# A sparse-attention and mixer kernel: PSUM as four double tiles, the MLP in 64-row halves, one relu per pair, scores unit by unit, mask constants through POOL's DMA queue

## The chip, the core and the metric

The kernel runs on one core of a Trainium2 chip. A core has TensorE (PE: matmuls, and weight loads that run beside them), VectorE (DVE), ScalarE (ACT), GpSimd (POOL) and SyncE (SP). PE writes to PSUM, which has eight banks of 512 float32 columns on 128 partitions; ACT and DVE read it from there[...]. SP and ACT issue DMAs to a hardware queue, POOL to a software queue. The metric is the device time in microseconds (us). Each engine takes its instructions in the order in which the program has them; engines wait for each other by semaphores.

## The reference

Four batches, eight heads, 768 positions, head size 64. Attention runs with a block mask (blocks of 32: neighbours, first and last block, and three sampled blocks per row), and its output x, put back to 768 x 512, goes through a low-rank mixer and an MLP:

```
scores = q k^T / 8, masked to -1e9;  attn = softmax(scores);  x = attn v
h = x^T U V          (U: 768 x 32, V: 32 x 768)
u = x + h^T
out = u + relu(u w1) w2      (w1: 512 x 2048, w2: 2048 x 512)
```

All results are float32; the kernel multiplies in float16 and accumulates in float32.

## The kernel before, in words

The work goes through 16 head pairs (four batches of four). A pair has nine units. A unit is 1024 columns of scores on 128 partitions (keys on partitions; two heads of 512 queries, or two heads of two times 256): `scores` (line 406) writes them to a PSUM tile `psc` of two banks, one `activation` with exp (line 419) turns them into the float16 tile `est`. In batches 1 to 3 a score matmul contracts over 64 rows: head 0 lies on partitions 0 to 63, head 1 on 64 to 127, and the two are issued one after the other, on different row halves of PE. In batch 0 the mask is added inside the matmul through one-hot rows, so its score matmuls have 128 rows; in later batches `mask_mul` (line 423) multiplies `est` by a 0/1 mask `m01` on DVE.

When a pair's nine units are done, `values` (482) multiplies est by v in 72 matmuls of 65 columns (the 65th is the sum of the row) into `pav`, in two halves of three query tiles; `norm` (446) takes the reciprocal and multiplies, to `xs` (float32), and POOL casts it to `xh`. `mix_a` (496) multiplies by U into `pa`, DVE copies that to `a16`; `mix_h_rows` (532) multiplies by V in 64-row halves into `ph`, DVE adds it to xs, giving u (`xf`), POOL casts it to `uh`, and a transposing DMA (`turn_u`, 551) makes `uT`.

The MLP of a batch (`mlp_steps`, 568) is a list of steps: 32 of `w1` (one tile `pt` of 384 columns: four matmuls with 128 rows, then a relu on ACT or DVE to `tT`) and 24 of `w2` (four of the 16 matmuls of 512 columns into `pch`; after the last, DVE adds u and SP sends the result out).

The order on PE is written out at build time. Batch 0 runs its own loop (line 782). Then 108 units follow in `groups`: eight groups of one unit, then groups of two. In each group the program issues the scores, then the tail work of earlier pairs, then MLP steps of the batch before: `run_fill` (798) spreads a batch's steps over the groups up to the next entry of `OPENS`, where the next batch's MLP begins (`LATE` = 8 groups after a batch's last scores). The last batch's MLP comes after everything else. Estimates of the engines' clocks (`clk`, `run_on`, `give_back`) choose the PSUM bank and the engine of each relu while the program is built.

PSUM is two `psc` tiles of two banks each (`pscp`) and four single banks (`psp`), from which all other tiles come: `pst_tile` takes the bank that is free first.

At the start, ACT's queue loads k's first part, `small_const` (mask constants), the identity and one-hot rows; SP's queue loads q's first part, `sampled_blocks`, the rest of q and k, and so on. `small_const` and `sampled_blocks` give `eq`, `cb` and `cbd` on DVE (lines 262 to 284), from which PE makes the mask rows (`pm`, line 299).

Of the kernel before, what the change touches and what calls it, by code (L numbers as in the profile page):

```python
# [21 lines left out]
def kernel(  # L22
# [63 lines left out]
    opool = ctx.enter_context(tc.tile_pool(name="opool", bufs=2))  # L86

    pscp = ctx.enter_context(
        tc.tile_pool(name="pscp", bufs=2, space=bass.MemoryType.PSUM)
    )  # L90
    psp = ctx.enter_context(
        tc.tile_pool(name="psp", bufs=1, space=bass.MemoryType.PSUM)
    )
# [9 lines left out]
    banks = [0.0] * 4  # L103
    pairs = {"pav": deque([0, 1]), "ps": deque([2, 3])}
    held = {}

    def pst_tile(shape, dtype, name, tag=None):
        if tag is None:
            n = min(range(4), key=lambda n: banks[n])
            clk["pe"] = max(clk["pe"], banks[n])  # L110
        else:
            n = pairs[tag][0]
            pairs[tag].rotate(1)
        t = psp.tile(shape, dtype, tag=f"bank{n}", name=name)
        banks[n] = OPEN
        held[id(t)] = (n, t)
        return t

    def give_back(t, when):
        banks[held.pop(id(t))[0]] = when + LAG  # L120
# [5 lines left out]
    def mm(out, lhsT, rhs, start, stop, loose=False, us=0.0):  # L126
        clk["pe"] += us
        keep(
            nc.tensor.matmul(  # L129
                out, lhsT, rhs, start=start, stop=stop, skip_group_check=loose  # L130
            )
        )

# [85 lines left out]
    keep(nc.vector.memset(Vd, 0.0))  # L219
# [4 lines left out]
    def hot_rows(eng, st, h, n):  # L224
# [3 lines left out]
    keep(nc.sync.dma_start(out=qld[:, :, 0:TQ], in_=q0[:, :, 0:TQ]))  # L228
    keep(nc.scalar.dma_start(out=kld[:, :, 0:TK], in_=k0[:, :, 0:TK]))
    keep(  # L230
        nc.sync.dma_start(
# [4 lines left out]
    keep(nc.scalar.dma_start(out=small[0:NB], in_=small_dr.ap()))  # L236
# [85 lines left out]
    pm0 = pscp.tile([P, 2, 512], FP32, tag="psc", name="pm")  # L322
    pm1 = pst_tile([P, QA], FP32, "pm", tag="pav")
    pm2 = pscp.tile([P, 2, 512], FP32, tag="psc", name="pm")
# [33 lines left out]
    mvld = w2t[0:R, 0:3, :].rearrange("r j d -> r (j d)").bitcast(FP32)  # L358
# [47 lines left out]
    def scores(i, u, est):  # L406
        psc = pscp.tile([P, 2, 512], FP32, tag="psc", name="psc")
# [10 lines left out]
        clk["pe"] = max(clk["pe"], exp_end[-2]) + 0.32  # L418
        keep(nc.scalar.activation(out=est, in_=psc, func=AF.Exp, scale=0.125))  # L419
        exp_end.append(run_on("act", 0.905))  # L420
        ready[id(est)] = exp_end[-1]

# [23 lines left out]
    def norm(i, c, pav, xs, xh, quick=False):  # L446
# [14 lines left out]
        def full():  # L461
            times(x3)
            give_back(pav, run_on("dve", 0.48))
# [15 lines left out]
    def new_pav(tag=None):  # L479
        return pst_tile([P, 3, 2, D + 1], FP32, "pav", tag)  # L480

    def values(i, c, ests, xs, xh):
        b, hp = divmod(i, HP)
        pav = new_pav()
        for h in range(2):
            for j in range(3):
                for g in range(T):
                    mm(
                        pav[:, j, h, :],
                        weights(ests, g, 3 * c + j, h),  # L490
                        vts[b % 2][:, 2 * hp + h, g, 0 : D + 1],
                        g == 0, g == T - 1, us=0.0315,
                    )
        norm(i, c, pav, xs, xh)

    def mix_a(i, xh, box, part, tag=None):
# [4 lines left out]
        if part == 1:  # L501
            box["a"] = misc.tile([P, P], FP16, tag="a16", name="a16")
            keep(nc.vector.tensor_copy(out=box["a"], in_=box["pa"]))
            give_back(box["pa"], run_on("dve", 0.2))

    def mix_h(i, c, a16, xs, uh, tag=None, quick=False):
# [14 lines left out]
        def full():  # L521
            plus(u3)
            give_back(ph, run_on("dve", 0.47))
# [8 lines left out]
    def mix_h_rows(i, a16, xs, uh):  # L532

        b, hp = divmod(i, HP)
        phs = [pst_tile([P, 3, P], FP32, "ph") for c in range(2)]
        for j in range(3):
            for c in range(2):
                mm(phs[c][:, j, :], Vd[rows[c], 3 * c + j, :], a16[rows[c]], True, True)
        clk["pe"] += 0.17
        for c in range(2):  # L540
            tc3 = slice(3 * c, 3 * c + 3)
            u3 = xfs[b][:, tc3, hp * P : (hp + 1) * P]
            keep(
                nc.vector.tensor_tensor(  # L544
                    out=u3, in0=xs[:, tc3, :], in1=phs[c], op=ALU.add
                )
            )
            give_back(phs[c], run_on("dve", 0.47))
            keep(nc.gpsimd.tensor_copy(out=uh[:, tc3, :], in_=u3))  # L549
# [9 lines left out]
    def turn_u_pe(i, uh, tag):  # L559
# [5 lines left out]
        give_back(pt, run_on("dve", 0.6))  # L565


    def mlp_steps(b):
# [3 lines left out]
        def w1(jj, c):  # L572
            if c == 0:
                tT[jj] = tpool.tile([P, S], FP16, tag="tT", name="tT")
            uT = uTs[b].rearrange("p n t s -> p n (t s)")
            pt = pst_tile([P, HS], FP32, "pt")
            for cc in range(NCC):
                mm(
                    pt,
                    w1t[:, cc, jj * P : (jj + 1) * P],  # L580
                    uT[:, cc, c * HS : (c + 1) * HS],
                    cc == 0, cc == NCC - 1, us=0.162,
                )
            dst = tT[jj][:, c * HS : (c + 1) * HS]
            ends = {e: max(clk[e], clk["pe"]) + d for e, d in (("act", 0.43), ("dve", 0.48))}
            if ends["act"] <= ends["dve"]:
                keep(nc.scalar.activation(out=dst, in_=pt, func=AF.Relu))  # L587
                give_back(pt, run_on("act", 0.43))
            else:
                keep(nc.vector.tensor_scalar_max(out=dst, in0=pt, scalar1=0.0))  # L590
                give_back(pt, run_on("dve", 0.48))

        pchs = {}

        def w2(sc, part, n0=0, n1=HD):
            if part == 0:
                pchs[sc] = pst_tile([P, n1 - n0], FP32, "pch")
            for jj in range(4 * part, 4 * part + 4):
                mm(
                    pchs[sc],  # L600
# [4 lines left out]
            if part == 3:  # L605
                of = opool.tile([P, n1 - n0], FP32, tag="of", name="of")
                keep(
                    nc.vector.tensor_add(out=of, in0=xfs[b][:, sc, n0:n1], in1=pchs[sc])  # L608
                )
                give_back(pchs[sc], run_on("dve", 0.6))  # L610
                keep(
                    nc.sync.dma_start(
                        out=out[b].rearrange("(p t) d -> p t d", t=T)[:, sc, n0:n1],
                        in_=of,
                    )
                )

        for jj in range(NJJ):
            for c in range(2):
                steps.append((0.65, lambda jj=jj, c=c: w1(jj, c)))  # L620
        for sc in range(T):
            cuts = [(0, HD)] if (b, sc) != (B - 1, T - 1) else [(0, 384), (384, HD)]
            for n0, n1 in cuts:
                for part in range(4):
# [3 lines left out]
                            lambda sc=sc, part=part, n0=n0, n1=n1: w2(sc, part, n0, n1),  # L628
                        )
# [46 lines left out]
    def turn_part(i, nm, part):  # L676
# [4 lines left out]
        if part == 1:  # L681
# [9 lines left out]
            give_back(pt, run_on("dve", 0.48))  # L691
# [11 lines left out]
    def at_unit(i, u):  # L703
        if (i, u) in MASKS:
            mask_tiles(MASKS.index((i, u)))
        if i == 0:
            if u == 0:
# [5 lines left out]
                for nm, o, pt, t in (("q", qa[0], pq, TQ), ("k", ka[0], pk, TK)):  # L713
                    for h in range(2):
                        half_copy(nc.vector.tensor_copy, o, h, pt, t, T)
                give_back(pq, 0.0)
                give_back(pk, 0.0)
                give_back(warm, 0.0)
                issue(2, "qk")
                cast(1, "q")  # L720
                cast(1, "k")
                cast(1, "v")
            if u == 1:
                for h in range(2):
# [220 lines left out]
```

The softmax here doesn't subtract the row's maximum and nothing guards it: scores larger than these inputs give would overflow.

## Time and profile before

| what | value |
|---|---|
| runs, median of 4 (lowest, highest) | 290.3 us (290.25, 290.73) |
| the profiled execution: its own time, its span | 290.27 us, 288.40 us |
| PE busy; weight loads busy | 281.1 us (97%); 162.8 us (56%) |
| DVE, ACT, POOL busy | 188.8 (65%), 177.9 (62%), 95.8 us (33%) |
| chain that ended last, by engine | PE 84%, ACT 11%, issue, DVE and DMA 1% each |
| matmuls of pt, pch, pav, psc | 512, 400, 1152, 384 |
| exp: est<-psc on ACT | 144 of 1023 ns |
| mask: est<-est,m on DVE | 108 of 834 ns on average |
| relu on ACT, on DVE | 82 of 495 ns, 46 of 547 ns |
| TensorE's granted clock | 1.0 after the first moments |

Matmuls are pipelined: the recorded duration of one (327 ns for 384 columns) reaches past the start of the next, so the time that PE needs is read from start to start. The chain that ended last goes back from the last instruction to what released it, step by step; its shares say where the span went. Weight loads (PEld) run beside matmuls.

### The profile page before, as it was taken

The numbers are of one execution on the slowest core, as the hardware profiler recorded it, in microseconds if no ns is written. First come the engines' busy times: TensorE is split into PE (matmuls) and PEld (weight loads), VectorE is DVE, ScalarE is ACT, GpSimd is POOL, SyncE is SP. The second block draws the span as 40 slices with busy tenths as digits, with TensorE's granted clock in tenths as the row PEclk, the third lists the DMA queues.
The fourth block names the chain that finished last, engine by engine and source line by source line (L and its number), as shares of the span: only waits on it lengthen the run. The fifth ranks groups of instructions, "written<-read, shape, count | busy, mean of one in ns | idle before, by whom it ended". The sixth has DMA issues, their size and how long they took to land.

```text
span 288.4 us, 6744 instructions
## 1 busy us (share of the span) xinstructions
PE 281.1 (97%) x2765; PEld 162.8 (56%) x2765; DVE 188.8 (65%) x347; ACT 177.9 (62%) x232; POOL 95.8 (33%) x126
## 2 busy tenths in 40 slices
PE   7999998999999999999999999999999999999996
PEld 2577775456646454556565645566564644665443
DVE  5767767889897888888887695779787522000112
ACT  3699999687795857577776554577865000776000
POOL 2559854106444464516144251603031201000000
PEclk9999999999999999999999999999999999999999
DMA  6999999962357677773444365161010223000112
GB/s 168 317 286 269 235 261 268 216 188 60 84 151 97 223 165 199 217 146 67 131 124 127 99 184 137 44 93 31 0 31 0 62 77 102 36 0 2 71 74 74
DMA packets 46414, 36.91 MB, mean 128 GB/s; under 512 B 27272, under 2 KB 42896, under 8 KB 46384
## 3 DMA queue, kind: packets, MB, share of 16 engines
q1 hardware_dynamic: 43208, 32.06, 41.3%
q0 software_dynamic: 2688, 4.19, 8.1%
q8 instruction: 21, 0.34, 0.5%
q10 hardware_dynamic: 488, 0.24, 0.3%
q14 instruction: 9, 0.07, 0.1%
HBM read 27.80 MB, written 6.29 MB: 118 GB/s over the span
## 4 chain that ended last, share of the span: by engine, by line
PE 84%; ACT 11%; issue 1%; DVE 1%; DMA 1%; ACTq 0%; DVEq 0%
PE pt L129 29%; PE pch L129 29%; PE psc L129 11%; ACT est L419 11%; PE pav L129 10%; PE pa L129 2%; DMA w1t<-small_const 1%; PE ph L129 1%; PE warm L129 1%; PE pturn L194 1%; PE pm L129 0%; PE pmk L129 0%; DVE uT L564 0%; DVE xh L453 0%; PE puT L563 0%
## 5 line engine op out<-in xcount | busy, mean ns | idle before, releaser
L419 ACT ACTIVATE est<-psc 128x1024 f16<-128x1024 f32 x144 | 138.6, 1023 | 45.9 <-PE psc L129 45.3
L129 PE MATMUL pt<-uT,w1t 128*128 128x384 f16 x512 | 89.1, 327 | 0.2 <-DVE uT L564 0.2
L129 PE MATMUL pch<-w2t,tT 128*128 128x512 f16 (+2 forms) x400 | 87.9, 371 | 0.0
L431 DVE TENSOR_TENSOR est<-est,m 128x1024 f16<-128x1024 f16 x108 | 85.4, 834 | 0.0
L129 PEld LDWEIGHTS <-w1t 128*128 128x128 f16 x512 | 47.6, 98 | 38.2 <-issue 8.6
L587 ACT ACTIVATE tT<-pt 128x384 f16<-128x384 f32 x82 | 39.3, 495 | 36.1 <-PE pt L129 34.9
L129 PEld LDWEIGHTS <-tT 128*128 128x128 f16 x400 | 36.4, 98 | 44.3 <-issue 5.4
L129 PEld LDWEIGHTS <-est 128*128 128x128 f16 x1152 | 44.0, 97 | 10.8 <-issue 0.5
L471 POOL CAST xh<-xs 128x384 f16<-128x384 f32 x30 | 21.4, 716 | 85.6 <-DVE xs L453 84.8
L608 DVE TENSOR_TENSOR of<-xf,pch 128x512 f32<-128x512 f32 (+2 forms) x25 | 16.5, 661 | 49.9 <-PE pch L129 49.8
L129 PE MATMUL pav<-vt,est 128*128 128x65 f16 x1152 | 46.4, 193 | 0.1
L129 PE MATMUL psc<-qT,kT 64*128 64x512 f16 (+1 forms) x288 | 33.9, 327 | 0.9 <-ACT est L419 0.8
L549 POOL CAST uh<-xf 128x384 f16<-128x384 f32 x24 | 16.1, 696 | 38.3 <-issue 33.6
L590 DVE TENSOR_SCALAR tT<-pt 128x384 f16<-128x384 f32 x46 | 24.2, 547 | 0.9 <-PE pt L129 0.7
L129 PE MATMUL psc<-qa,ka 128*128 128x512 f16 (+1 forms) x96 | 21.6, 327 | 0.3
L453 DVE TENSOR_TENSOR xs<-pav,rcp 128x384 f32<-128x384 f32 x32 | 17.8, 557 | 1.9
L448 DVE RECIPROCAL rcp<-pav 128x6 f32<-128x6 f32 x32 | 6.2, 194 | 19.4 <-PE pav L129 18.9
L188 POOL CAST kst<-kld 128x768 f16<-128x768 f32 x15 | 16.5, 1100 | 4.3 <-DMA kld<-in_k_dram 4.3
L129 PEld LDWEIGHTS <-kT 64*128 64x128 f16 x288 | 10.2, 94 | 13.4 <-issue 8.8
L182 POOL CAST vt<-vld 128x768 f16<-128x768 f32 x16 | 15.6, 973 | 5.4 <-DMA vld<-in_v_dram 4.5
L188 POOL CAST qst<-qld 128x768 f16<-128x768 f32 x15 | 16.5, 1101 | 2.2 <-PE psc L129 1.6
L544 DVE TENSOR_TENSOR xf<-xs,ph 128x384 f32<-128x384 f32 x24 | 12.2, 548 | 4.5 <-PE ph L129 4.5
(57 smaller groups left out, 113.8 us busy)
## 6 DMA issues: line engine op xcount, KB each, us to landing
vld<-in_v_dram SPq DMA_DIRECT2D x16, 384.0 KB, 4.5
out_dram<-of SPq DMA_DIRECT2D x23, 256.0 KB, 2.2
qld<-in_q_dram SPq DMA_DIRECT2D x15, 384.0 KB, 4.5
kld<-in_k_dram SPq DMA_DIRECT2D x15, 384.0 KB, 4.0
w1t<-in_moe_w_ch_dram POOLq DMA_DIRECT2D x4, 512.0 KB, 9.8
w2t<-in_moe_w_ch_dram POOLq DMA_DIRECT2D x4, 512.0 KB, 18.4
qld<-in_q_dram SPq DMA_DIRECT2D x1, 256.0 KB, 3.2
kld<-in_k_dram SPq DMA_DIRECT2D x1, 256.0 KB, 4.2
```

Source lines behind the costliest of these rows:

```text
L129: nc.tensor.matmul(out, lhsT, rhs, start=start, stop=stop, skip_group_check=loose)
L182: nc.gpsimd.tensor_copy(out=vts[b % 2][:, 2 * hp : 2 * hp + 2, :, 0:D], in_=ld)
L188: keep(nc.gpsimd.tensor_copy(out=st.rearrange("p t h d -> p h t d"), in_=ld))
L419: keep(nc.scalar.activation(out=est, in_=psc, func=AF.Exp, scale=0.125))
L431: keep(nc.vector.tensor_tensor(out=o, in0=o, in1=m, op=ALU.mult))
L453: nc.vector.tensor_tensor(out=o.rearrange("p j (h d) -> p j h d", h=2), in0=pav[:, :, :, 0:D], in1=rcp[:, :, :, None].broadcast_to([P, 3, ...
L471: keep(nc.gpsimd.tensor_copy(out=xh[:, 3 * c : 3 * c + 3, :], in_=x3))
L544: nc.vector.tensor_tensor(out=u3, in0=xs[:, tc3, :], in1=phs[c], op=ALU.add)
L549: keep(nc.gpsimd.tensor_copy(out=uh[:, tc3, :], in_=u3))
L587: keep(nc.scalar.activation(out=dst, in_=pt, func=AF.Relu))
L590: keep(nc.vector.tensor_scalar_max(out=dst, in0=pt, scalar1=0.0))
L608: nc.vector.tensor_add(out=of, in0=xfs[b][:, sc, n0:n1], in1=pchs[sc])
```

## The change

What it does, part by part.

- PSUM: batch 0 has two double tiles of two banks (as before) and two pools of two single banks (`pav`, `ps`). Early in batch 1 (groups 6 and 7) the two single pools are closed and become two more double tiles. From then on scores, MLP pairs, values, `pa` and `ph` all take one of four doubles, the one that the planner's clocks say is free first.
- MLP of batches 0 to 2: each 128-row matmul is two of 64 rows. The two column halves (c = 0, 1) of a pair have a bank each. In phase 0, rows 0 to 63 go to bank 0 and rows 64 to 127 to bank 1; in phase 1 it is the other way round. Before phase 1, `half_wait` makes PE wait for the last matmul of phase 0 (in the built program the wait sits on the first weight load of phase 1). One relu of 768 columns per pair. `run_fill` ends a group's steps ahead of a phase 1, unless it is the group's first step. The last batch's MLP keeps 128 rows, with paired tiles and one relu per pair.
- Values: one double tile and one normalisation for a pair instead of two halves; `mix_a_rows` in 64-row halves (two sums in two banks, added on DVE); `mix_h_rows` into one double, with one add and one cast.
- Groups: one unit each; `LATE` = 14; tail steps at groups 0, 3 and 6 after a pair's last mask, instead of 0, 1, 3 and 5.
- Start: `sampled_blocks` and `small_const` are issued by POOL, first in its queue, instead of by SP and ACT. The copies of the mask rows for the second buffer (`qa`, `ka`) are issued in unit 0 instead of unit 1, ahead of pair 2's q and k. V of the mixer is loaded to two row halves; DVE's memset of `Vd` goes.
- Output: `of` holds two row tiles (one buffer instead of two), sent in one DMA in batches 0 to 2.

```diff
+    first = {
+        nm: tc.tile_pool(name=nm + "p", bufs=1, space=bass.MemoryType.PSUM, side=side)
+        for nm, side in (("ps", "left"), ("pav", "right"))
+    }
...
+    def double(name, n=None):
+        if n is None:
+            n = min(doubles, key=lambda n: doubles[n][1])
+            assert doubles[n][1] < OPEN
+            clk["pe"] = max(clk["pe"], doubles[n][1])
+        pool = doubles[n][0]
+        t = pool.tile([P, 2, 512], FP32, tag=f"double{n}", name=name)
+        doubles[n] = (pool, OPEN)
+        held[id(t)] = (n, t)
         return t
...
+    def half_wait(ins):
+        nop = nc.tensor.nop()
+        tc.add_manual_dep(
+            nop.ins, ins.ins.name,
+            mybir.DependencyInfo(mybir.DependencyClass.Sync, mybir.DependencyReason.DATA),
+            reason="halves",
+        )
+        keep(nop)
...
-    keep(nc.vector.memset(Vd, 0.0))
...
+    keep(
+        nc.gpsimd.dma_start(
+            out=sbi[0:NB].rearrange("z r w -> z (r w)"),
+            in_=sampled_blocks.bitcast(I32),
+        )
+    )
+    keep(nc.gpsimd.dma_start(out=small[0:NB], in_=small_dr.ap()))
...
-        psc = pscp.tile([P, 2, 512], FP32, tag="psc", name="psc")
+        psc = double("psc", len(exp_end) % 2 if i < HP else None)
...
+    def mix_a_rows(xh, box):
+
+        pa = double("pa")
+        for sc in range(T):
+            for r in range(2):
+                mm(
+                    pa[:, r, 0:P], Ut[rows[r], sc, :], xh[rows[r], sc, :],
+                    sc == 0, sc == T - 1, us=0.027,
+                )
+        a16 = box["a"] = misc.tile([P, P], FP16, tag="a16", name="a16")
+        keep(nc.vector.tensor_copy(out=a16, in_=pa[:, 0, 0:P]))
+        keep(nc.vector.tensor_tensor(out=a16, in0=a16, in1=pa[:, 1, 0:P], op=ALU.add))
...
-        def w1(jj, c):
-            if c == 0:
+        def w1(jj, phase, by_rows):
+            if phase == 0:
                 tT[jj] = tpool.tile([P, S], FP16, tag="tT", name="tT")
+                pair[0] = double("pt")
             uT = uTs[b].rearrange("p n t s -> p n (t s)")
-            pt = pst_tile([P, HS], FP32, "pt")
+            pt = pair[0]
+            if by_rows and phase == 1:
+                half_wait(pair[2])
             for cc in range(NCC):
...
+                for r in ((0, 1), (1, 0))[phase] if by_rows else (0,):
+                    c = r ^ phase
+                    rr = rows[r] if by_rows else slice(0, P)
+                    last = mm(
+                        pt[:, c, 0:HS],
+                        w1t[rr, cc, jj * P : (jj + 1) * P],
+                        uT[rr, cc, c * HS : (c + 1) * HS],
+                        cc == 0 and not (by_rows and phase),
+                        cc == NCC - 1 and not (by_rows and not phase),
+                        by_rows, us=0.081 if by_rows else 0.162,
+                    )
+            if by_rows and phase == 0:
+                pair[2] = half_done(last)
+            if phase == 1:
+                relu(tT[jj], pt)
...
+        while fill and state["debt"] > 0:
+            if fill[0][2] and n and us < 1e6:
+                break
...
-    groups = [[x] for x in stream[:SINGLE]]
-    groups += [stream[n : n + 2] for n in range(SINGLE, len(stream), 2)]
-    LATE = 8
+    groups = [[x] for x in stream]
+    LATE = 14
...
+        if gi == 6:
+            more_doubles("pav", 2)
+        if gi == 7:
+            more_doubles("ps", 3)
...
-                for at, fn in zip((0, 1, 3), steps):
-                    work.append((gi + at, fn))
-                beside.append((gi + 5, steps[3]))
+                work.append((gi, steps[0]))
+                work.append((gi + 3, steps[1]))
+                beside.append((gi + 6, steps[2]))
```

`w2_rows` does for w2 what `w1` does with `by_rows`: phase 0 and phase 1, of four steps each, for two output tiles in the two banks of one double, with the same `half_wait` ahead of phase 1.

## The prediction

> **What bounds the kernel now.** I read the chain that ended last first. From about 46 us on it hardly leaves TensorE (PE 84% of the span in all); before that it is the exponentials on ScalarE. In order of time it ends so (start, duration, what):
>
> ```profile
> 234.79 1.94 PE pch L129 x9
> 236.74 0.27 PE ph L129 x6
> 237.01 7.01 PE pch L129 x32
> 244.02 20.80 PE pt L129 x128
> 264.82 20.77 PE pch L129 x112
> 285.60 0.02 issue
> 285.62 0.29 DVE of L608
> ```
>
> The last batch's MLP alone is 41.6 us of matmuls without a gap: 20.80/128 = 162.5 ns for each 384-column matmul. That is the price of pure streaming. Next, the busy time by stages (length; busy of PE, weight loads, DVE, ACT, POOL; clock, DMA):
>
> ```profile
> 9.30:46.00 36.70, 36.24 (x514) 26.27 (x512) 25.89 (x57) 35.43 (x38) 25.48 (x39) 1.00 1.08 269
> 46.00:49.60 3.60, 2.70 (x31) 1.63 (x28) 3.09 (x8) 3.35 (x5) 1.37 (x2) 1.00 1.16 267
> 49.60:244.00 194.40, 193.05 (x1966) 109.49 (x1964) 149.56 (x260) 120.30 (x154) 66.77 (x77) 1.00 0.46 115
> 244.00:286.00 42.00, 41.58 (x241) 22.67 (x238) 4.96 (x8) 15.68 (x32) 0.00 (x0) 1.00 0.10 38
> ```
>
> Batch 0 (9.3 to 46) is ScalarE's: 35.4 of 36.7 us. From 49.6 to the end PE is busy and DVE (77%) and ACT (62%) are not full. So 236 us of the span are worth exactly what PE's stream is worth. But "busy" hides losses inside the stream; the timeline of PE shows them (start, duration, group):
>
> ```profile
> 57.53 0.61 PE L129 MATMUL psc<-qT,kT 64*128 64x256 f16 x6
> 58.07 2.12 PE L129 MATMUL pt<-uT,w1t 128*128 128x384 f16 x12
> 60.12 0.61 PE L129 MATMUL psc<-qT,kT 64*128 64x512 f16 x6
> 60.66 0.66 PE L129 MATMUL pt<-uT,w1t 128*128 128x384 f16 x3
> ```
>
> From start to start: 12 pt take 60.12 - 58.07 = 2.05 us, but 12 x 0.1625 = 1.95. The six score matmuls are three pairs that run at once on rows 0-63 and 64-127: 512 + 2 x 256 columns, 0.43 us of streaming, and they take 0.54. So every change between 128-row and 64-row matmuls costs about 0.10 us, each way. In the single starts of the trace it is 96 ns nearly everywhere, whatever the neighbours (pav, pt, pch, psc), and after a change to 64 rows the first pair takes 10 ns more. Between groups of one row count it is 0: six pch and then pav start 1.29 us apart, which is 6 x 0.2158.
>
> Sum for 49.6 to 286 from these starts: streaming 221 us, 108 changes 10.4 us, pav's small overhead (about 2 ns each) 2 us, everything else 2.7 us. In that rest are three waits for a PSUM tile, at 54.1 (0.74), 68.9 (0.26) and 107.1 (0.70), and one of 0.32 at 49.8 for uT.
>
> **The change part by part.** The sum is made against the profiled execution, 290.27 us (span 288.40, and 1.87 around it); the median of the runs is 290.3, so no correction.
>
> *Row changes removed.* With the MLP of batches 0 to 2, mix_a and mix_h all in 64-row halves beside the scores, only the values (pav) stay at 128 rows. Counted in the program's order: 128 changes before, 48 after. The 20 ahead of the first MLP tile stay; 108 become 28. 80 x 0.096 + 40 x 0.010 = **-8.1 us**, all of it on PE's path.
>
> *Streaming of the halves.* 384 w1 and 288 w2 matmuls each become two of 64 rows; columns streamed stay the same (257.8 us in both programs). Here a rule speaks against the change: the Trainium skill, "TensorE: Matmul & The Clock Gate", section "LDWEIGHTS (loading the stationary operand)", says that a load takes its columns / 1.2 GHz whatever the number of rows. Two loads of 128 columns would be 213 ns, more than the 162 ns that a w1 pair streams: 384 x 51 ns = +19.7 us (an estimate from that page), and the change would lose. The trace differs: two 64-row psc pairs of 256 columns follow each other in 109 ns, with two loads each, and ph pairs of 128 columns in 56 ns; both are the streaming time alone. The loads of the two halves run at once. I take 0; bounds 0 to +2.
>
> *The waits between the phases.* half_wait makes a weight load wait until PE's own last matmul of phase 0 has finished, because phase 1 writes each bank from the other row half. All PE work behind it is held. There are 57. No row shows this wait alone. A 384-column matmul is recorded at 327 ns, a 512-column one at 379, and ScalarE starts about 40 ns after such an end (psc ends 10.04, est starts 10.08). So phase 1 may start 0.37 us after the last pair of phase 0 began (0.42 in w2). In the program's order 56 of the 57 have at least one score unit (0.216) or pa (0.335) in between, which brings PE to 0.162 + 0.216 = 0.378 (0.432). The wait ends about as its cover does. The loads can't run ahead, so I take 20 ns each, as after a row change; 1.1 us, and 0.2 for the one with no cover: **+1.3**; bounds 0 and +11.6 (0.2 each, no cover at all).
>
> *PSUM, ACT and DVE.* Four double tiles serve scores, MLP pairs, pav, pa and ph. One relu per pair saves ACT and DVE time: ACT 1023 ns for 1024 columns and 495 for 384 give about 0.81 for 768, against 2 x 0.495; DVE by the same way 0.97 against 1.09. Over the 48 pairs of batches 0 to 2 these engines are spared some 7 us, worth nothing where PE is the bound. But a tile comes free later: a pair's half isn't freed until its relu is over. In the first MLP, nine units now take about 13.7 us of PE; ACT needs 9 x 0.905 (exps start 0.90 apart: instructions overlap by 0.12 on ACT, 0.08 on DVE) + 5 relus x 0.7 = 11.7, DVE nine masks at 0.75 + three relus at 0.88 + 2.4 for norm, a16 and xf = 11.8. That is 86% of each, in order, on few buffers: stalls of a tenth here and there, and more where a mask takes 1.3 us beside a POOL cast. I take **+2.0**, bounds 0 and +6. Scores singly no longer ask for two PSUM tiles at once, so the waits at 68.9 and 107.1 go: **-1.0** (bounds -1.0, 0). The wait at 54.1 stays: pturn now waits for the put-off xf adds on DVE.
>
> *Tail of a pair.* mix_a comes three single units after pav, about 3.2 us in the w2 stretch. Its input needs rcp 0.23, one 768-wide multiply about 0.9, one POOL cast about 1.1 and three hops: 2.5 us if DVE is free, up to 3.4 behind a mask. Fusing the two halves delays the first. **+0.6**, bounds 0 and +3.
>
> *Start.* small_const heads the chain: 3.40 us from its issue at 1.26 to landing, then eq, cbd, pm, and so the first scores at 9.34. POOL has nothing queued until 4.23 and issues a DMA in 0.55 to 0.75 (w1t, w2t rows). Two of them from 0.7 end near 2.0, and 2 to 2.4 us to landing (out_dram rows: 2.2) gives 4.0 to 4.4 instead of 4.66. ACT and SP each lose an issue in front of id16 and the second halves of q and k. Batch 0 follows the shift since exp is its bound: **-0.4**, bounds -0.9 and +1.0. Against it: on SP, the four qa/ka copies (0.6 each) now stand ahead of q and k of pair 2, which issue near 11.5 instead of 6.7. They are cast at 13.94 and 16.24 and wanted by PE near 20 to 21, so a delay of up to 4 us is covered; the second moe_V load and two more Ut copies (0.35 each) lie beside exp as well. 0, bounds 0 and +1.0.
>
> *Last MLP and output.* It stays at 128 rows; the add waits on an output DMA only 3.45 us old or older (2.2 to land), the last two adds on none. 0. Removing Vd's memset (0.38 on DVE, at 2.88, idle after it): 0.
>
> Sum: -8.1 + 1.3 + 2.0 - 1.0 + 0.6 - 0.4 = -5.6, so **284.7 us**.
>
> **The rivals.** (1) The likeliest, above: PE stays the bound and most of the row changes' price is gained. For it: 96 ns in every one of the 108 places, and pairs that stream at full rate. With the stalls between 0 and +4 it gives 282 to 287.5. Chance 0.70.
>
> (2) PE becomes one that waits: with tiles held through whole pairs and ACT and DVE at 86%, PSUM waits and late xh eat most of the gain: stalls at their upper ends, +6 and +3 instead of +2.0 and +0.6: 284.7 + 6.4 = 291, or with half of that excess 288. For it: before, one late exp already cost 0.70 at a stroke. Against it: from 120 to 244 PE lost under 0.4 us in 20 to anything but row changes at the same load. As 287.5 to 289.7: chance 0.13.
>
> (3) Slower, by one thing: the 57 waits between phases. If a PE load held by PE's own semaphore resumes only after the array is empty and the score pairs in between don't cover it, each costs some 0.2 us (0.366 - 0.162): 11.6 us, 10.3 more than I took: 295.0. It decides against the change from about 0.12 us each (1.3 + 5.6 = 6.9 over 57). Against it: 56 of 57 have a cover as long as the wait. With rival 2's remainder: chance 0.12, 290.9 to 296.
>
> (4) That it doesn't do what it says (row halves not paired, since the order of banks and rows in phase 1 breaks the overlap): each half would stream alone, 384 x 0.162 + 288 x 0.216 = +124 us; the pairs of psc and ph speak against it. Chance 0.02, with 0.03 left for no change.
>
> **How the numbers follow.** 284.7 is the likeliest. The range takes in rival 1 whole and reaches to rival 2's end: 281.5 to 289.5, leaving out about 0.17. A measurement of this kernel tells about 0.2% (0.6 us) from no change. Faster: 0.70 + 0.13 = 0.83; same 0.03; slower 0.14.
>
> **What would show it.** Right: pt and psc groups next to each other with no 0.10 between their starts; 0.10 only around pav; the first weight load of a phase 1 right at the end of the score pair; the last MLP starting near 238.5 instead of 244.0, and again 41.6 us long; small_const landed by 4.4. Wrong: PE idle ahead of psc or pt, put down to ACT or DVE; gaps of 0.1 or more in front of every phase 1; 64-row pt pairs further apart than 0.163; first scores later than 9.3.

## The result, and the profile after

The median of 31 runs is 289.3 us (288.2 to 290.4), against 290.4 for the kernel before (51 runs, 289.6 to 292.0). The ratio is 0.995, 95% interval 0.994 to 0.996: 1.1 us faster, where 5.6 were forecast. The profiled execution of after is among its shortest: 288.38 us (span 286.6), 1.9 under that of before. About half of the executions of after have a mean granted clock of 0.994 and a median of 288.5 us, as the profiled one has, and the others 1.0 and 289.6.

The chain that ended last, of the kernel after, from the tail of the third batch's MLP on (start, duration, what):

```profile
227.31 3.56 PE pch L146 x32
230.87 0.34 PE pa L146 x12
231.21 2.59 PE pch L146 x24
...
238.35 3.63 PE pch L146 x32
241.97 20.91 PE pt L146 x128
262.88 20.77 PE pch L146 x112
283.66 0.02 issue
283.68 0.29 DVE of L680
```

The last MLP is as long as before, 41.7 us. It starts 2 us earlier (from the matmul records 241.9 instead of 243.9); 238.5 was forecast. So all that is missing lies ahead of it. The stretch from the first pt matmul to the start of the last MLP is called the steady stretch from here on: 194.4 us before, 191.2 after. The timeline of PE, kernel after, at a quiet place (start, duration, group):

```profile
126.30 0.40 PE L146 MATMUL psc<-qT,kT 64*128 64x512 f16 x2
126.54 0.82 PE L146 MATMUL pt<-uT,w1t 64*128 64x384 f16 x8
127.20 0.38 PE L146 MATMUL psc<-qT,kT 64*128 64x256 f16 x4
127.42 0.81 PE L146 MATMUL pt<-uT,w1t 64*128 64x384 f16 x8
128.07 0.38 PE L146 MATMUL psc<-qT,kT 64*128 64x512 f16 x2
```

Here the change does what it was to do. Eight pt halves are four pairs, 4 x 0.1625 = 0.65 us of streaming; the next psc starts 0.66 us after they begin (127.42 - 126.54 = 0.88 with 0.22 of psc). No 0.10 is left between the groups, the halves run at once, and a phase 1 behind one score pair waits some 11 ns.

The losses are elsewhere. First, PE's idle times from 56 to 236 us, kernel after (engine, tile and line, what it waited for: total us, times, longest):

```profile
PE psc L146 <- DVE of L680: 1.2, 2, 1.0
PE psc L146 <- DVE tT L648: 1.1, 2, 0.7
PE pav L146 <- DVE est L465: 0.6, 2, 0.4
PE pt L146 <- DVE tT L648: 0.5, 2, 0.3
PE pt L146 <- DVE xf L605: 0.2, 1, 0.2
```

The view counts from the recorded end of a matmul, which reaches past the start of the next one; from start to start the waits are longer (the account below). The same view of the kernel before has one line:

```profile
PE psc L129 <- ACT est L419: 0.5, 1, 0.5
```

Every line of after names DVE. By engine, DVE now carries 16% of the chain that ended last; before it was 1%.

Second, the start: POOL's queue in the kernel after (start, duration, engine and line, what; in brackets the idle time before).

```profile
1.28 0.69 POOL L260 DMA_DIRECT2D sbi<-in_sampled_blocks_dram  x1 [0.84 <-POOLq L1053]
1.97 0.55 POOL L265 DMA_DIRECT2D w1t<-small_const  x1
```

and what the chain says of it:

```profile
1.97 4.05 DMA w1t<-small_const
6.91 0.71 PE pm L146 x3
```

small_const lands at 6.02. Before it landed at 4.66; 4.0 to 4.4 was forecast. The mask rows (pm) come at 6.91 instead of 5.42, the first exponential at 11.25 instead of 10.08, and batch 0, which runs at exp's pace, ends as much later (first pt matmul at 50.67 instead of 49.49).

This execution shows the start at its best, because PE was fast early. The first warm-up matmuls, of 512 columns, start 0.43 us apart, where 0.22 is the rate later. Here the pm matmuls at 6.91 already run at 0.22, and 0.43 returns only from 8.45 to 10.6, where the granted clock is 0.50 (7.8 to 11.1). The kernel before ran at 0.43 up to about 9.3. Five of the runs below begin with the same code as after. Two of them (no break, no casts of v) look like it: mean granted clock 0.994, first pt matmul at 50.80 to 50.82. In the other three (mask at 0.9, 128-row MLP, norm later) the mean is 1.0 and PE was at 0.43 until at least 11 us: there the first exponential comes at 11.85 to 11.96 and the first pt matmul at 51.45 to 52.13, 2.0 to 2.6 us later than before instead of 1.2. No trace of after itself with a mean of 1.0 is kept. With the steady stretch 3.1 shorter, such a range of starts would explain why the medians differ by only 1.1 and the profiled executions by 1.9.

The account below is from start to start in PE's records (streaming is 0.4167 ns a column plus 2.5 ns a matmul, which gives both the 162.5 ns measured for 384 columns and the 215.8 for 512):

| us | before | after | difference |
|---|---|---|---|
| first pt matmul at | 49.49 | 50.67 | +1.2 |
| row changes after it, 96 ns each | 10.4 (108) | 2.6 (27) | -7.8 |
| PE waits over 60 ns | 2.2 | 6.7 | +4.5 |
| streaming, and all small gaps with pav's overhead | 181.8 | 181.9 | +0.1 |
| last MLP starts at | 243.86 | 241.91 | -2.0 |

### The profile page after: what moved, and what is told of

The parts are those of the page before. It is cut to its first block, busy times and chain, and to the rows that moved or that the text cites. A ratio compares the mean times of both kernels' runs of the same rounds, so it can differ in the third digit from the quotient of the medians.

```text
span 286.6 us, 8065 instructions
## 1 busy us (share of the span) xinstructions
PE 275.0 (96%) x3509; PEld 165.6 (58%) x3509; DVE 189.7 (66%) x290; ACT 175.2 (61%) x191; POOL 90.7 (32%) x106
## 4 chain that ended last, share of the span: by engine, by line
PE 78%; DVE 16%; ACT 2%; DMA 1%; issue 1%; POOL 0%; DVEq 0%; ACTq 0%; POOLq 0%
PE pch L146 27%; PE pt L146 21%; PE pav L146 13%; PE psc L146 11%; DVE est L465 8%; ACT est L452 2%; DVE xs L533 2%; DVE tT L648 2%; DMA w1t<-small_const 1%; PE pturn L226 1%; PE pa L146 1%; PE ph L146 1%; DVE of L680 1%; PE warm L146 1%; PE pmk L146 1%
## 5 line engine op out<-in xcount | busy, mean ns | idle before, releaser
L146 PE MATMUL pt<-uT,w1t 64*128 64x384 f16 (+1 forms) x896 | 94.1, 324 | 0.9 <-DVE tT L648 0.5
L146 PE MATMUL pch<-w2t,tT 64*128 64x512 f16 (+3 forms) x688 | 91.4, 372 | 0.1
L146 PEld LDWEIGHTS <-w1t 64*128 64x128 f16 (+1 forms) x896 | 48.4, 95 | 35.4 <-PE pt L146 4.4
L146 PEld LDWEIGHTS <-tT 64*128 64x128 f16 (+1 forms) x688 | 38.4, 95 | 38.9 <-PE pch L146 1.9
L645 ACT ACTIVATE tT<-pt 128x768 f16<-128x768 f32 x41 | 33.3, 812 | 27.3 <-PE pt L146 27.2
L146 PEld LDWEIGHTS <-est 128*128 128x128 f16 x1152 | 41.7, 97 | 11.6 <-issue 4.9
L680 DVE TENSOR_TENSOR of<-xf,pch 128x1024 f32<-128x1024 f32 (+3 forms) x16 | 15.2, 951 | 43.5 <-PE pch L146 43.5
L541 POOL CAST xh<-xs 128x768 f16<-128x768 f32 x12 | 13.6, 1130 | 70.1 <-DVE xs L533 44.5
L613 POOL CAST uh<-xf 128x768 f16<-128x768 f32 x12 | 13.7, 1142 | 54.1 <-DVE xf L605 27.2
L648 DVE TENSOR_SCALAR tT<-pt 128x768 f16<-128x768 f32 x23 | 21.8, 946 | 0.6 <-PE pt L146 0.4
L214 POOL CAST vt<-vld 128x768 f16<-128x768 f32 x16 | 16.4, 1025 | 4.6 <-DMA vld<-in_v_dram 4.6
L531 DVE RECIPROCAL rcp<-pav 128x12 f32<-128x12 f32 x12 | 2.8, 232 | 19.9 <-PE pav L146 19.9
L533 DVE TENSOR_TENSOR xs<-pav,rcp 128x768 f32<-128x768 f32 x12 | 11.5, 958 | 1.6 <-DVE rcp L531 0.5
```

The costliest lines, as they stand in the source:

```text
L146: ins = nc.tensor.matmul(out, lhsT, rhs, start=start, stop=stop, skip_group_check=loose)
L214: nc.gpsimd.tensor_copy(out=vts[b % 2][:, 2 * hp : 2 * hp + 2, :, 0:D], in_=ld)
L533: nc.vector.tensor_tensor(out=xs.rearrange("p (c j) (h d) -> p c (j h) d", c=2, h=2), in0=pv[:, :, :, 0:D], in1=rcp[:, :, :, None].broadca ...
L541: keep(nc.gpsimd.tensor_copy(out=xh, in_=xs))
L613: keep(nc.gpsimd.tensor_copy(out=uh, in_=u))
L645: keep(nc.scalar.activation(out=o, in_=i, func=AF.Relu))
```

## The experiments

The losses have two places, and I put two questions. Is the start lost to the software queue alone? And why does PE wait for DVE: because DVE has too much work (masks dearer than the planner thinks, slowed by POOL's casts), because it stands idle in its own order, or because of the waits between the phases? Unless said otherwise, each edit is on the kernel after, times are compared with its median (289.3), and "the waits" are PE's waits over 60 ns from the first pt matmul to the last MLP (6.7 us in after).

**Constants by the hardware queues.**

```
-    keep(nc.gpsimd.dma_start(out=sbi..., in_=sampled_blocks...))
-    keep(nc.gpsimd.dma_start(out=small[0:NB], in_=small_dr.ap()))
     keep(nc.sync.dma_start(out=qld[:, :, 0:TQ], ...))
     keep(nc.scalar.dma_start(out=kld[:, :, 0:TK], ...))
+    keep(nc.sync.dma_start(out=sbi..., in_=sampled_blocks...))
+    keep(nc.scalar.dma_start(out=small[0:NB], in_=small_dr.ap()))
```

> The changed kernel with one part undone: sampled_blocks and small_const are issued by SP and ACT again, as before the change. In the profile of the changed kernel small_const lands at 6.0 us instead of 4.7, and the first exp starts at 11.25 instead of 10.08. If the start is what moved, the first exp comes back to 10.1 and the time falls by 1.1 to 1.4 us, to about 288.0. If the late constants are covered by ScalarE's later work (batch 0 is its), or if id16 and q's second half now come late instead, the time stays within 0.3 us of the changed kernel's 289.3.

Measured: 287.9 us (287.5 to 288.3, 6 runs), ratio to before 0.991 (0.989 to 0.993); 1.4 under the kernel after. The first scores are back at 9.41. The waits are as in after (6.7). But in the profiled execution the first pt matmul is at 50.58, not near 49.5: two exponentials of batch 0, the 16th and the 20th, start 0.5 and 0.4 us late. That is only 0.1 us ahead of the profiled execution of after, whose PE was fast early; this run's PE was at 0.43 up to about 9.4, and against the three runs with a late PE (51.45 to 52.13) it gains 0.9 to 1.5. So the queue cost 1.4 us of the median, though little in the one execution of after that is kept, and about a microsecond of the start is still lost, which is taken up below.

**The planner told that a mask takes 0.9 us** instead of 0.6, which moves 16 relus from DVE (23 to 7) to ACT (41 to 57).

```
-        run_on("dve", 0.6, ready[id(est)])
+        run_on("dve", 0.9, ready[id(est)])
```

> The changed kernel, but the planner is told that a mask takes DVE 0.9 us instead of 0.6 (the profile: 0.88 on average). Nothing else is edited; by this the planner moves 16 of the 23 relus of DVE to ACT. Theory A (DVE falls behind: norm, masks and relus in one queue, so PSUM tiles come free late): PE's waits for DVE in the steady part, 6.6 us in the changed kernel against 1.9 before, fall to 3 or less, and the time to about 286. Theory B (four tiles are too few for what is held at once, whoever empties them): the waits move from DVE to ACT, exps come later, and the time stays at 289 or rises by up to 1 us.

Measured: 287.3 us (5 runs), ratio 0.989 (0.987 to 0.991), 2.1 under after, between what the two theories gave. The waits fall from 6.7 to 4.1 us and the steady stretch from 191.2 to 188.8; now 1.1 us of the idle times in the view are for ACT's exps. Two of DVE's groups from 56 to 236 us in this run (line, engine, operation, names, shapes, count | busy us, mean ns | idle us just before, and for what):

```profile
L648 DVE TENSOR_SCALAR tT<-pt 128x768 f16<-128x768 f32 x7 | 6.7, 952 | 1.6 <-PE pt L146 1.6
L531 DVE RECIPROCAL rcp<-pav 128x12 f32<-128x12 f32 x12 | 2.8, 232 | 25.3 <-PE pav L146 25.3
```

The relus on DVE fall from 21.8 to 6.7 us, and the time in which DVE stands in front of its reciprocals grows from 19.9 to 25.3: a third of what was spared is lost there again, and the rest still brings 2.1 us. So DVE's lateness causes PE's waits, and the amount of DVE's work has a part in it; some of the waiting goes over to ACT when ACT takes the work.

**The MLP of batches 0 to 2 with 128 rows**, all else as in after (`by_rows` for `b < 0` instead of `b < B - 1`).

> The changed kernel with the MLP of batches 0 to 2 at 128 rows (four double tiles, one relu per pair and single scores stay). Changes between 128 and 64 rows rise from 48 to 228, the waits between phases go. At 96 ns each and 10 ns after each change to 64 rows that is +18 us, less 1 for the waits: about 306. If PE's waits for DVE hide part of it (PE would be late anyway, and a slower PE gives DVE time), +13 to +15: 302 to 304. If row changes cost nothing in this place, 288.

Measured: 301.4 us (4 runs), ratio 1.038 (1.036 to 1.040). From the first pt on there are 208 changes of rows instead of 27: 20.0 us against 2.6, +17.4. But the steady stretch is only 12.6 us longer, because all other gaps fall from 7.9 to 3.2 us, and the waits among them from 6.7 to 1.0. The price of a change holds at 181 places. And the waits are not a property of DVE's work alone: DVE stands 19.4 us in front of eleven reciprocals here too, and with a slower PE that is covered. They are what a faster PE runs into.

**No break ahead of a phase 1**: `run_fill` may begin a group's steps with a phase 1, so that 21 of the waits between phases have no score unit to cover them instead of one.

```
-            if fill[0][2] and n and us < 1e6:
-                break
```

> The changed kernel, but the steps of a group are not cut off ahead of a phase 1. 21 of the 57 phase-1 starts then follow their phase 0 with nothing in between, instead of 1. In the changed kernel a covered start costs 11 ns over its cover. If an uncovered one costs what the matmul's recorded length says (0.37 less 0.162, about 0.2 us), the 20 cost 4 us: 293. If a stall of PE gives time to DVE, which is late anyway, less: 291. If an uncovered wait costs a row change (0.1), 291.3 at most.

Measured: 290.9 us (17 runs), ratio 1.002 (1.0005 to 1.0035), 1.6 over after. Each bare wait shows 0.23 to 0.24 us more between the starts; 20 of them are 4.6 us, of which fewer waits for DVE give a part back. A covered one costs 11 ns. So these waits are dear, and in the kernel after they are hidden as forecast: they are not where the gain is lost.

**Norm one group later.** The reciprocal and the multiply go behind the next group's mask in DVE's order; the last two lines of the edit stand in the loop over groups, right after its masks.

```
     def values(i, ests, xs, xh):
...
+        def norm_later():
             rcp = misc.tile([P, 2, 6], FP32, tag="rcp", name="rcp")
             keep(nc.vector.reciprocal(out=rcp, in_=pv[:, :, :, D]))
...
+        norms.append(norm_later)
...
+        while norms:
+            norms.popleft()()
```

> The reciprocal and the multiplication that norm the values are put one group later in VectorE's order, after the next group's mask; nothing else moves. Theory A, VectorE stands in its own order: it idles 1.66 us a pair (19.9 us in twelve) before the reciprocal, waiting for the 72 pav matmuls, while masks that could run are queued behind, and what it then owes makes TensorE wait: the idle time before the reciprocal falls to under 0.8 us a pair, TensorE's waits over 60 ns from 6.7 to about 4 us, the time to 286.5. Theory B, VectorE has simply too much work in the stretches with six masks and a relu: the waits stay at 6 to 7 us, or grow for the PSUM bank pair held a microsecond longer, and the time is 289 to 290.

Measured: 286.7 us (5 runs), ratio 0.984 (0.982 to 0.987), 2.6 under after: theory A to within 0.2. The waits fall to 3.6 and the steady stretch to 188.2, 3.0 less than in after. What it mends shows in DVE's groups from 62 to 102 us, where the first MLP runs. First the kernel after:

```profile
L465 DVE TENSOR_TENSOR est<-est,m 128x1024 f16<-128x1024 f16 x27 | 23.8, 923 | 0.0
L648 DVE TENSOR_SCALAR tT<-pt 128x768 f16<-128x768 f32 x6 | 5.7, 946 | 0.1
L531 DVE RECIPROCAL rcp<-pav 128x12 f32<-128x12 f32 x2 | 0.5, 232 | 3.6 <-PE pav L146 3.6
```

DVE is busy 35.55 of these 40 us. Of the rest, 3.6 stand in front of two reciprocals, and the masks never wait (0.0): their exps are always done before DVE comes to them, up to 4.2 us before in this stretch. (The kernel before shows 0.0 for its masks too; what is new is that PE is held up by it.) For nearly 2 us a pair DVE stands still. In each of the eleven pairs that have a mask behind the reciprocal, the exp of the first one had ended 2.0 to 3.0 us before the reciprocal began; that of the second ended 1.35 us or more after. So one mask of about 0.8 us could have run in each wait, not several. In the run with the norm later:

```profile
L465 DVE TENSOR_TENSOR est<-est,m 128x1024 f16<-128x1024 f16 x25 | 21.5, 892 | 1.2 <-ACT est L452 1.0
L535 DVE RECIPROCAL rcp<-pav 128x12 f32<-128x12 f32 x3 | 0.7, 232 | 3.7 <-PE pav L146 3.7
```

The wait per reciprocal falls from 1.8 to 1.2 us, masks start at most 1.75 us after their exps, and some now wait for ACT: DVE has caught up. Over 56 to 236 us the idle time before the twelve reciprocals goes from 19.9 to 12.9, which leaves 1.1 us a pair where under 0.8 was expected. The masks also became shorter there, 886 to 801 ns, 8.9 us of DVE's time in all (why isn't shown), so the run alone doesn't separate order from work.

**Casts of v left out after the first batch** (the later batches use the first batch's values), which takes 10 us of work from POOL.

```
         if nm == "v":
+            if b > 0:
+                return
...
-                            vts[b % 2][:, 2 * hp + h, g, 0 : D + 1],
+                            vts[0][:, 2 * hp + h, g, 0 : D + 1],
```

> GpSimd's casts of v are left out after the first batch (1.18 us each, nine in the steady part), and the later batches use the values of the first: this leaves a part of the computation out. Theory A, masks are slow (886 ns beside 680 alone) because GpSimd's casts run beside them, and this is what fills VectorE: GpSimd's busy time falls by 18%, the masks' mean by about 35 ns to 850, VectorE's work by 3.6 us over the steady part, and the time by about 1 us to 288.3. Theory B, it is not the casts but the order of the queue: masks fall as much or not, and the time stays within 0.4 us of 289.3.

Measured: 289.4 us (6 runs), ratio 0.994 (0.991 to 0.996): no change from after. The masks fell to 856 ns, as expected, and spared DVE 3.1 us. Its groups from 56 to 236 us in this run:

```profile
L465 DVE TENSOR_TENSOR est<-est,m 128x1024 f16<-128x1024 f16 x104 | 87.8, 886 | 0.1
L531 DVE RECIPROCAL rcp<-pav 128x12 f32<-128x12 f32 x12 | 2.8, 232 | 19.9 <-PE pav L146 19.9
```

are those of after; and without the casts of v:

```profile
L467 DVE TENSOR_TENSOR est<-est,m 128x1024 f16<-128x1024 f16 x104 | 84.7, 856 | 0.1
L533 DVE RECIPROCAL rcp<-pav 128x12 f32<-128x12 f32 x12 | 2.8, 233 | 22.2 <-PE pav L146 22.2
```

DVE finishes its masks earlier and then stands longer in front of the reciprocal (22.2 instead of 19.9). PE's waits don't move (6.6). Time saved on DVE ahead of the reciprocal is given back there, and theory A falls. So 3 us less of masks bring nothing while the order stays, where 15 us less of relus (mask at 0.9) brought 2.1; for the norm later, the order is the likelier cause than its shorter masks, though 8.9 us of them without the order weren't tried.

**The rest of the start, first try: U's copies on DVE.** Spreading U over `Ut` takes four copies on POOL since the change (1.50 us; 0.64 before), ahead of the casts of xh and uh. On top of the constants by the hardware queues, the four copies go to DVE.

> The constants again by the hardware queues, as in the first experiment, and the four copies that spread U over Ut (2 us of GpSimd's queue in the first batch, twice as many as before the change) done by VectorE. Theory A, the start is lost twice, first to the late constants and, once these are mended, to GpSimd's longer copies, which hold back the casts of xh and uh: first scores at 9.4, first paired MLP matmul back near 49.6 (50.6 in the first experiment), 1.0 us under the first experiment: 286.9. Theory B, the first batch ends late for the changed order of SP's queue (the copies of qa and ka ahead of the loads of pair 2): the first paired MLP matmul stays near 50.5 and the time at 287.9.

Measured: 291.0 us (12 runs), ratio 1.001 (0.999 to 1.004): 3 us worse than with the constants alone, which neither theory had. DVE's timeline in that run shows the first part of it:

```profile
19.63 2.35 DVE L877 CAST Ut<-w2t 64x192 f16<-64x192 f32 x4 [0.29 <-DMA w2t<-in_moe_U_dram]
22.01 0.20 DVE L482 RECIPROCAL rcp<-pav 128x6 f32<-128x6 f32 x1
22.24 0.56 DVE L487 TENSOR_TENSOR xs<-pav,rcp 128x384 f32<-128x384 f32 x1
```

The copies take 2.35 us on DVE, start only when U lands at 19.6, and the norm of the first values stands behind them; ACT's exps stand still for 2.05 us ahead of 24.68. From 24.0 to 27.4 the granted clock is then 0.50 in this execution, and ACT waits another 1.2 us for PE's scores. The first pt matmul is at 53.39. So in this execution some two of the three us are the copies' own; what lowered the clock isn't shown.

**Second try: only the half of U that batch 0 doesn't need later** (two of the four copies one pair later, still on POOL), constants by the hardware queues.

> The constants by the hardware queues, as in the first experiment; of GpSimd's four copies that spread U over Ut, the two for the second 64 columns, which nothing in the first batch needs, go one pair later. Theory A, GpSimd's longer queue (0.75 us more at 19.8) holds back xh, uh and with them two exponentials of the first batch (0.48 and 0.39 us): first paired MLP matmul at 49.7, 0.9 us under the first experiment's 50.6, time 287.0. Theory B, the order of SP's queue, which this kernel keeps, does it: first paired MLP matmul near 50.5, time 287.9.

Measured: 288.2 us (6 runs), ratio 0.992 (0.989 to 0.994); first pt at 50.43. That is no gain over the constants alone (287.9), so theory A fails. POOL has 0.75 us less to do, but in this execution U landed at 20.5, and xh is cast at 22.8, no earlier than with the constants alone (22.9; 21.8 in the kernel before). The first exponential was 2 us earlier here (8.10), and nearly all of it was lost by the 16th (24.66 against 24.79).

**Start and norm together.** Second try plus norm one group later.

> The run before (start mended both ways) and the norm of the values one group later, together. If the start and VectorE's order are two separate losses, their gains add: 289.3 - 1.4 - 2.6 and, if GpSimd's copies were the rest of the start, - 0.9, which is 284.4; the stretch from the first paired matmul to the last MLP is 188.2 as in the run with the norm alone. If they overlap, it is 285.5 to 286.5.

Measured: 284.8 us (6 runs), ratio 0.981 (0.977 to 0.985). The two losses add, as expected but for the part of the copies; the steady stretch is 188.2 us, and the last MLP starts at 238.75.

**The same, and a mask at 0.8 for the planner**, which moves 11 more relus to ACT (41 to 52).

> As the run before, and the planner's price of a mask 0.8 instead of 0.6, near the 0.801 that a mask took with the norm one group later. Theory A, what is left of TensorE's waits (3.6 us over 60 ns) is still VectorE's backlog: more relus go to ScalarE and the waits fall to about 2.5, the time to 283.3. Theory B, with the norm out of the way VectorE has room and the waits left are those of the start of the second batch (1.4 us) and the steps of the tail: the time stays within 0.4 us of the run before.

Measured: 284.7 us (6 runs), ratio 0.981 (0.978 to 0.983): nothing on top, theory B. With the norm out of the way it no longer matters where the relus go. The waits are 3.7.

**SP's queue in the order of before** (loads of q and k of pair 2 ahead of the qa and ka copies), on the kernel of the run "start and norm together".

> As the ninth run (constants by the hardware queues, second half of U later, norm one group later), and SP's queue again in the order of the kernel before: the loads of q and k of pair 2 ahead of the four copies into the rows of qa and ka. Theory A, that order is what was left of the start: U's load lands at 19.7 instead of 20.5, the 16th and 20th exponential are no longer held back, the first paired MLP matmul is at 49.6 or earlier (50.56 in the ninth run), the time 283.9. Theory B, the transfers up to U's load are bound by what the DMA engines move, whatever their order: U's load lands within 0.3 us of 20.5 and the time stays at 284.8.

Measured: 285.3 us (4 runs), ratio 0.981 (0.979 to 0.983), first pt at 51.08. Theory A fails: U lands no earlier but at 21.1. SP's timeline in this run:

```profile
12.78 1.76 SPq L859 DMA_DIRECT2D w2t<-in_moe_V_dram  x2
16.41 0.35 SPq L861 DMA_DIRECT2D w2t<-in_moe_U_dram  x1
```

Asked for earlier, the loads of pair 2 stand ahead, and SP issues V's at 12.8 and U's only at 16.4 (14.4 without the edit). That is nearer to theory B (the transfers are bound by what is to be moved), though U came 0.6 later than theory B has it.

**And V and U ahead of v of pair 2.**

> As the run before, and the loads of V and U ahead of that of v of pair 2 (384 KB). If the casts of U and V on GpSimd, which wait for these loads, hold back the first batch (by either theory), they come 1 us earlier or more, no exponential waits at the 16th and 20th, and ScalarE's pace alone sets the first batch: the first paired MLP matmul 1 to 2 us before 50.56, at 48.6 to 49.6, the time 282.9 to 283.9. If something else holds xh back, the time stays at that of the run before.

Measured: 285.2 us (6 runs), ratio 0.982 (0.979 to 0.984). U's copies start at 20.25, xh is cast at 22.55, and the first pt is at 50.19, 0.4 us earlier than in the run with start and norm; the time is the same within the runs. POOL now stands 2.9 us in front of a cast of v. What is left of the start, some 0.7 us against before, lies in the chain of loads and casts around U, which the change made longer (four copies, V twice); these runs don't tell POOL's share from the transfers'. That stays open.

## Why the gain was forecast too high

The step that failed first is "PSUM, ACT and DVE", with "Tail of a pair": +2.0 - 1.0 + 0.6 = +1.6 was put down for the waits, and +4.5 was measured (0.2 of it the bare wait between phases, forecast elsewhere). The prediction had the load nearly right and drew the wrong conclusion from it: 11.8 of 13.7 us, "stalls of a tenth here and there". What it put at nothing is the time in which DVE is blocked. The reciprocal stands in DVE's order and waits for the 72 pav matmuls, 1.66 us a pair (19.9 / 12). An estimate from its own numbers: 11.8 + 1.66 = 13.5 of 13.7, a full queue. And masks took 923 ns from 62 to 102 us, 0.84 with the overlap of 0.08, not 0.75: nine times 0.09 more, 14.3 of 13.7. So in such stretches DVE falls behind, and PE waits at the next tile that DVE must give back. The kernel before has nearly the same wait at the reciprocal, from 56 to 236 us:

```profile
L448 DVE RECIPROCAL rcp<-pav 128x6 f32<-128x6 f32 x24 | 4.7, 194 | 18.4 <-PE pav L129 18.2
```

But its PE spent 8 us more on row changes, and that hid it. The run with 128-row MLP shows it (waits 1.0), the norm one group later removes 3.1 of the 4.5 us of added waits, and fewer casts don't, since what they save is lost at the reciprocal again. That the work counts beside the order is shown by the run with the mask at 0.9 (waits 4.1). The two mends overlap: eleven relus more on ACT bring nothing once the norm stands later.

The second is "Start": -0.4 forecast, +1.2 measured in the profiled execution and 2.0 to 2.6 in three runs with the same start and a late PE; the hardware queues give 1.4 back. Two terms were off, and how long PE stays slow was not counted. POOL doesn't issue from 0.7 but from 1.28, and small_const lands 4.05 us after its issue, where 2 to 2.4 was taken from rows of other DMAs in the middle of the program (out_dram). The start's own row, 3.40 us for the same tensor by the hardware queue, was nearer and was passed over.

What held: row changes -8.1, measured -7.8 (27 left instead of 28, 96 ns each). Halves stream side by side at full rate: 178.9 us of streaming in both programs, so the trace decided rightly, and not the rule of the Trainium skill ("TensorE: Matmul & The Clock Gate", section "LDWEIGHTS (loading the stationary operand)"), from which the estimate was +19.7. In the kernel after the halves' loads overlap two by two:

```profile
L146 PEld LDWEIGHTS <-w1t 64*128 64x128 f16 x768 | 36.0, 94 | 26.8 <-PE pt L146 4.4 <-issue 2.0 <-DVE xs L533 0.4
```

768 loads of 94 ns would be 72.2 us one after the other; the loading side was busy for 36.0.

The waits between phases: +1.3 taken; 56 at 11 ns and one at 0.23 are 0.8. Its rival, 0.2 each, is what a wait without cover costs (0.23), so the cover is what made the change gain at all. The two waits of psc for ACT's exp are gone. The last MLP is unchanged. The order of SP's queue, taken at 0, isn't what holds the start, as far as the run with the loads first shows. But the chain around U, with the two more Ut copies that "lie beside exp as well", is hidden behind exp only as long as the constants are late: with those mended, xh comes at 22.9 instead of 21.8, and two exponentials wait.

So the second rival, PE as one that waits, with 287.5 to 289.7, is what came to pass in its number, and in PE that waits; the mechanism is DVE's queue, with the reciprocal in it, rather than tiles held by whole pairs. With start and norm mended the time is that of the forecast, 284.8 against 284.7, but partly by luck: the first pt matmul comes at 50.56 where 49.1 was forecast, and the steady stretch takes 188.2 where the forecast comes to 189.2.

## What to carry to other kernels

An engine's load is its busy time plus the time in which its oldest instruction waits while work behind it is ready; read both from the groups (busy, and idle before) before calling 86% enough. When the bound engine gets faster, the others' old waits come out: price them at the new pace, not by how they looked beside the old one. And let an instruction that waits for a long block stand behind the work that is ready, which is a small edit here and was worth more (2.6 us) than the whole change (1.1). Last, a single profiled execution can lie a microsecond off the median by its start alone; the stretch behind the start is the steadier measure.

## What the runs showed of the hardware

- PE waiting for its own last matmul costs 0.23 us with nothing between, 0.01 with 0.22 us of other work between.
- A change between 64-row and 128-row matmuls costs 96 ns each way, in 27 to 208 places alike.
- A small DMA through POOL's software queue took 4.05 us from issue to landing, of which its packets moved only from 4.48 on (2.0 us after the issue had ended); the same tensor through ACT's hardware queue took 3.40.
- The same warm-up matmuls of 512 columns start 0.43 us apart in the first 4 us of every trace kept, and 0.22 apart later. The change came by 5.3 us in the run with U's second half later, which brought the first exponential 2 us forward against the run with the hardware queues; at 9.3 in the kernel before; after 13.2 in the run with the norm later. In the kernel after it came by 6.9, and 0.43 returned from 8.45 to 10.6. The granted clock reads 1.00 over the slow first stretch (before, 0 to 9.5) and 0.50 only over the later one (after, 7.8 to 11.1).
